# Block-sparse attention and hardswish MLP on one core: q and k cast by DMA in long runs with per-head transposes, one ordered load queue, and row sums from 8 KB rows

## Chip, cores, metric

The kernel runs on one core of a Trainium2 chip. The metric is the device time of the whole launch in microseconds (us), the median of several runs. The medians and ranges take in every run.

The profile's engine names: PE is TensorE's matmuls, PEld its weight loads, ACT is ScalarE, DVE is VectorE, POOL is GpSimd, SP is SyncE. L229 is line 229 of that kernel's own source, so one code line has different numbers in different kernels.

## The reference, cut to what matters

```python
batch, n_heads, seq, head_dim = (4, 8, 768, 64)
block, window = (32, 16)
k_sum = k.reshape(B, H, nb, block, D).max(axis=3)      # block summaries: max of keys,
v_sum = v.reshape(B, H, nb, block, D).mean(axis=3)     # mean of values
# softmax over the local band |i-j| < 16 together with the 24 block summaries
# (whose scores get log(block) added), times [v, v_sum]
...
h = x @ w_in                                           # x: 3072 x 512, d_ff = 2048
g = h * clip(h + 3, 0, 6) / 6
return (g @ w_out).astype(float32)
```

The MLP is cut into 8 tiles of 384 tokens, two per batch. The first layer of a tile is 64 matmuls ("hp", 16 steps of 4), the second 48 ("op").

## The kernel before, the parts that matter

q and k of batches 0 to 2 come as fp32 through the SyncE queue in 512-byte runs (two tokens of 256 bytes side by side in one partition), are cast on ACT and DVE, and are transposed on TensorE, six 128x128 transposes for a pair of heads. Since each partition holds two neighbouring tokens, the transposed PSUM tile has all even tokens first and then all odd ones. The copies out of PSUM put them back in order. Row sums of v come from four accumulating DMAs for each batch and head group, each of which waits for the one before it (51.0 us of GpSimd's waits in the trace are for DMAs of v rows).

```python
NSPLIT = 3; TSUM = 8
def load_split(b, p):                                   # SyncE queue, fp32
    ...
    nc.sync.dma_start(out=t, in_=src[b, 2*p:2*p+2].rearrange("h (u p s) d -> p (h u) (s d)", p=128, s=2))

def load_vrows(b, c):                                   # c = 0..3, accumulating, GpSimd queue
    for g in range(2):
        ...
        nc.gpsimd.dma_start(out=vr_t[b, g][:], in_=src[c], accum_op=ALU.bypass if c == 0 else ALU.add)

def vsum(b, g):
    nc.vector.tensor_reduce(a[:], vr_t[b, g][:].rearrange("p t d -> p d t"), axis=AX.X, op=ALU.add)
    ...

def Tk(b, p):
    tp = transposed(kb_t[b, p], ...)                    # 6 transposes into PSUM
    for j, copy in enumerate((nc.scalar.copy, nc.vector.tensor_copy)):
        rows = slice(64 * j, 64 * j + 64)
        o = kbd[p][rows, :, 64 * j:64 * j + 64]
        if b < NSPLIT:
            copy(o.rearrange("p n (c s) -> p s n c", s=2), tp[rows].rearrange("p (s n c) -> p s n c", s=2, n=NK))
    ...
```

The softmax here doesn't subtract the row's maximum and nothing guards it: scores larger than these inputs give would overflow.

## Time and profile before

| | |
|---|---|
| time, median (7 runs in the rounds of the first experiments) | 289.0 us |
| span of the profiled run | 287.4 us |
| TensorE busy | 236.1 us |
| first matmul of MLP tile 0 / 1 / 2 | 41.5 / 87.5 / 117.9 us |

The tile starts are read from the order of TensorE's matmuls: every 64th "hp" matmul opens a tile. From the page of the kernel before, its busy times and the chain that ended last (shares of the span):

```profile
PE 236.1 (82%) x1670; PEld 138.7 (48%) x1696; DVE 164.7 (57%) x357; ACT 167.1 (58%) x325; POOL 71.8 (25%) x109
...
PE 53%; DMA 22%; DVE 10%; issue 6%; ACT 4%; POOL 3%; POOLq 0%; ACTq 0%; DVEq 0%
PE op L311 22%; PE hp L301 21%; DMA vr<-in_v_dram 14%; DMA wout<-in_moe_w_out_dram 6%; DVE g L305 2%; DMA split<-in_k_dram 2%; DVE kbd L209 2%; PE num L273 2%; DVE red L213 2%; PE num L271 1%; DVE va L188 1%; ACT r L304 1%; PE den L280 1%; PE den L277 1%; PE sl L235 1%
```

The view of stretches of the kernel before, one line for each stretch in us, with the busy time and number of instructions of each engine, the granted share of TensorE's clock, the DMA share and GB/s:

```profile
0.00:41.50 41.50, 17.97 (x151) 13.23 (x152) 25.90 (x77) 22.76 (x43) 22.83 (x46) 1.00 1.20 205
41.50:100.00 58.50, 38.60 (x266) 22.64 (x268) 31.97 (x67) 28.62 (x58) 22.57 (x31) 0.82 1.09 183
100.00:287.40 187.40, 179.53 (x1257) 102.83 (x1278) 106.79 (x214) 115.71 (x226) 26.40 (x34) 1.00 0.42 64
```

TensorE is busy 96% of the time after 100 us. Before that it idles for 43 us, and that is the room that a change of the loads can win. (The 1.00 of the clock column in the first stretch is no measurement. The trace has no clock record before 39 us, and a 128x384 matmul of line 280 took 0.53 us at 38.5 us and 0.33 to 0.34 from 40.3 us on, so TensorE ran slower there.) The reads of v rows hold 14% of the chain.

The groups of instructions that the change touches (line, engine, operation, out<-in, shapes, count | busy us, mean ns | idle before and its releaser):

```profile
L209 DVE COPY kbd<-tp 64x768 bf16<-64x768 bf16 x12 | 12.1, 1011 | 11.8 <-ACT kbd L209 11.6
L209 ACT COPY kbd<-tp 64x768 bf16<-64x768 bf16 x12 | 12.0, 1000 | 3.1 <-PE tp L199 3.1
...
L188 DVE TENSOR_REDUCE va<-vr 96x64 f32<-96x512 f32 x8 | 8.2, 1026 | 7.3 <-DMA vr<-in_v_dram 7.3
L225 DVE COPY qT<-tp 128x768 bf16<-128x768 bf16 x8 | 8.1, 1011 | 0.0
...
L211 ACT COPY kbd<-tp 64x768 bf16<-64x768 bf16 x4 | 3.1, 787 | 0.4 <-PE tp L199 0.4
...
L211 DVE COPY kbd<-tp 64x768 bf16<-64x768 bf16 x4 | 2.2, 561 | 1.6 <-ACT kbd L211 1.6
```

### The profile page before, as it was taken

The numbers are of one execution on the slowest core, as the hardware profiler recorded it, in microseconds if no ns is written. First come the engines' busy times: TensorE is split into PE (matmuls) and PEld (weight loads), VectorE is DVE, ScalarE is ACT, GpSimd is POOL, SyncE is SP. The second block draws the span as 40 slices with busy tenths as digits, with TensorE's granted clock in tenths as the row PEclk, the third lists the DMA queues.
The fourth block names the chain that finished last, engine by engine and source line by source line (L and its number), as shares of the span: only waits on it lengthen the run. The fifth ranks groups of instructions, "written<-read, shape, count | busy, mean of one in ns | idle before, by whom it ended". The sixth has DMA issues, their size and how long they took to land.

```text
span 287.4 us, 4536 instructions
## 1 busy us (share of the span) xinstructions
PE 236.1 (82%) x1670; PEld 138.7 (48%) x1696; DVE 164.7 (57%) x357; ACT 167.1 (58%) x325; POOL 71.8 (25%) x109
## 2 busy tenths in 40 slices
PE   1433398167279999999999999999999999999994
PEld 1232265033135655555565555556665555555541
DVE  6773654326087996788868444776753444444400
ACT  3743768044337796746776667666876654555421
POOL 8234932032655413660423203000000000000000
PEclk9999999687859999999999999999999999999999
DMA  7999999999998699990659509010100101010111
GB/s 213 231 232 209 142 201 209 217 241 229 137 155 133 133 169 255 121 111 36 74 63 77 65 36 93 1 41 36 39 0 36 39 36 39 36 38 36 39 74 73
DMA packets 67350, 31.23 MB, mean 109 GB/s; under 512 B 39040, under 2 KB 61568, under 8 KB 67328
## 3 DMA queue, kind: packets, MB, share of 16 engines
q0 software_dynamic: 45056, 15.21, 46.7%
q1 hardware_dynamic: 22272, 15.73, 19.8%
q8 instruction: 13, 0.21, 0.3%
q14 instruction: 9, 0.07, 0.1%
HBM read 33.55 MB, written 6.29 MB: 139 GB/s over the span
## 4 chain that ended last, share of the span: by engine, by line
PE 53%; DMA 22%; DVE 10%; issue 6%; ACT 4%; POOL 3%; POOLq 0%; ACTq 0%; DVEq 0%
PE op L311 22%; PE hp L301 21%; DMA vr<-in_v_dram 14%; DMA wout<-in_moe_w_out_dram 6%; DVE g L305 2%; DMA split<-in_k_dram 2%; DVE kbd L209 2%; PE num L273 2%; DVE red L213 2%; PE num L271 1%; DVE va L188 1%; ACT r L304 1%; PE den L280 1%; PE den L277 1%; PE sl L235 1%
## 5 line engine op out<-in xcount | busy, mean ns | idle before, releaser
L301 PE MATMUL hp<-x,win 128*128 128x384 bf16 x512 | 108.5, 336 | 21.5 <-DVE g L305 21.2
L304 ACT ACTIVATE r<-hp,half_c 128x384 f32<-128x384 f32 x128 | 73.9, 579 | 63.5 <-PE hp L301 63.0
L311 PE MATMUL op<-wout,g 128*128 128x512 bf16 x358 | 97.7, 382 | 1.4 <-issue 0.2
L305 DVE SCALAR_TENSOR_TENSOR g<-r,hp 128x384 bf16<-128x384 f32 x128 | 70.0, 549 | 46.6 <-ACT r L304 46.0
L301 PEld LDWEIGHTS <-win 128*128 128x128 bf16 x512 | 49.0, 100 | 59.4 <-issue 28.8
L311 PEld LDWEIGHTS <-g 128*128 128x128 bf16 x384 | 37.5, 99 | 32.5 <-issue 1.4
L117 POOL DMA_DIRECT2D vr<-in_v_dram x32 | 25.0, 821 | 57.2 <-DMA vr<-in_v_dram 51.0
L107 POOL DMA_DIRECT2D vbd<-in_v_dram x32 | 26.3, 879 | 28.2 <-PE num L273 20.5
L291 DVE TENSOR_TENSOR x<-num,lg 128x384 bf16<-128x384 f32 x32 | 17.7, 554 | 21.5 <-ACT lg L290 20.8
L289 ACT ACTIVATE lg<-den 128x384 f32<-128x384 f32 x32 | 15.6, 492 | 15.9 <-PE den L287 9.5
L235 PE MATMUL sl<-qT,kbd 128*128 128x94 bf16 x192 | 15.7, 225 | 10.5 <-ACT asum L248 6.4
L238 ACT ACTIVATE at<-sl 128x376 bf16<-128x376 f32 x48 | 21.6, 483 | 2.1 <-PE sl L235 2.1
L95 ACT CAST qb<-split 128x384 bf16<-128x384 f32 x24 | 11.2, 513 | 17.9 <-DMA split<-in_q_dram 17.9
L235 PEld LDWEIGHTS <-kbd 128*128 128x128 bf16 x192 | 13.1, 110 | 17.2 <-issue 10.5
L199 PE MATMUL tp<-ident,kb 128*128 128x128 bf16 x96 | 9.8, 247 | 12.6 <-DVE kb L95 12.6
L315 ACT COPY ot<-op 128x512 f32<-128x512 f32 x24 | 13.9, 581 | 8.8 <-PE op L311 8.6
L209 DVE COPY kbd<-tp 64x768 bf16<-64x768 bf16 x12 | 12.1, 1011 | 11.8 <-ACT kbd L209 11.6
L239 DVE TENSOR_TENSOR at<-at,mask 128x376 bf16<-128x376 bf16 x48 | 15.7, 350 | 2.6 <-ACT at L238 2.3
L290 ACT ACTIVATE lg<-lg 128x384 f32<-128x384 f32 x32 | 16.8, 524 | 0.8
L273 PEld LDWEIGHTS <-vbd 128*128 128x128 bf16 x224 | 13.6, 101 | 6.6 <-issue 3.0
L95 DVE CAST kb<-split 128x384 bf16<-128x384 f32 x24 | 8.7, 388 | 13.2 <-DMA split<-in_k_dram 13.1
L273 PE MATMUL num<-at,vbd 128*128 128x94 bf16 (+2 forms) x224 | 14.9, 204 | 0.0
(64 smaller groups left out, 204.6 us busy)
## 6 DMA issues: line engine op xcount, KB each, us to landing
vr<-in_v_dram POOLq DMA_DIRECT2D x32, 192.0 KB, 6.2
out_dram<-ot SPq DMA_DIRECT2D x24, 256.0 KB, 2.0
split<-in_k_dram SPq DMA_DIRECT2D x12, 384.0 KB, 10.3
split<-in_q_dram SPq DMA_DIRECT2D x12, 384.0 KB, 11.2
vbd<-in_v_dram POOLq DMA_DIRECT2D x32, 96.0 KB, 4.6
win<-in_moe_w_in_dram POOLq DMA_DIRECT2D x4, 512.0 KB, 10.4
wout<-in_moe_w_out_dram POOLq DMA_DIRECT2D x4, 512.0 KB, 19.7
qb<-in_q_dram POOLq DMA_DIRECT2D x8, 96.0 KB, 3.2
```

Source lines behind the costliest of these rows:

```text
L95: copy(o[:, s], r[:, s])
L107: nc.gpsimd.dma_start(out=vbd[p][j * 64:(j + 1) * 64, :, j * 64:(j + 1) * 64], in_=v[b, 2 * p + j].rearrange("(n p) d -> p n d", p=KB))
L117: nc.gpsimd.dma_start(out=vr_t[b, g][:], in_=src[c], accum_op=ALU.bypass if c == 0 else ALU.add)
L209: copy(o.rearrange("p n (c s) -> p s n c", s=2), tp[rows].rearrange("p (s n c) -> p s n c", s=2, n=NK))
L235: nc.tensor.matmul(sp[:, i * WIN:(i + 1) * WIN], kbd[p][:, t], qT[p][:, t * KB:t * KB + WIN], start=True, stop=True)
L238: nc.scalar.activation(a, sp[:, 0:n * WIN].rearrange("p (n c) -> p n c", c=WIN), AF.Exp, scale=scl)
L273: nc.tensor.matmul(num[:, lo:hi], vbd[p][:, t], a[:, t, off:off + hi - lo], start=False, stop=(i == len(bl) - 1))
L291: nc.vector.tensor_tensor(xt[s][:, p], num[:], lg[:], op=ALU.mult)
L301: nc.tensor.matmul(hp[:], w_in_sb[:, kt, ft * 128:(ft + 1) * 128], xt[t][:, kt], start=(kt == 0), stop=(kt == NP - 1))
L304: nc.scalar.activation(r[:], hp[:], AF.Relu, bias=half_c[:], scale=1.0 / 6.0)
L305: nc.vector.scalar_tensor_tensor(gt[t][:, ft], r[:], 1.0, hp[:], op0=ALU.min, op1=ALU.mult)
L311: nc.tensor.matmul(ops[t][:], gt[t][:, ft, ts * 128:(ts + 1) * 128], w_out_sb[:, ft], start=(ft == 0), stop=(ft == NFT - 1))
```

## The change

Its intent: longer DMA runs for q and k of batches 0 and 1 (one partition holds 8 neighbouring tokens, 2 KB of fp32, cast to 1 KB of bf16 by the DMA), no fp32 staging and no casts on ACT and DVE, no accumulating reads that wait for each other, and one GpSimd queue whose order is fixed by hand so that what is needed first comes first. Batch 2 goes over to the 256-byte loads that batch 3 had before. The core of the diff:

```diff
-NSPLIT = 3
-TSUM = 8
+NLONG = 2
+RUN = 8
+RP = 96
+QCUT = 480
...
+    def load_k(b, p):
+        t = ld.tile([RP, 2, RUN, D], BF16, tag="kb", name="kb")
+        nc.gpsimd.dma_start(out=t[:], in_=k[b, 2 * p:2 * p + 2].rearrange("h (p s) d -> p h s d", s=RUN))
...
-            nc.gpsimd.dma_start(out=vr_t[b, g][:], in_=src[c], accum_op=ALU.bypass if c == 0 else ALU.add)
+        vr_t[b, g] = ld.tile([RS, BLK, D], F32, tag="vr", name="vr", bufs=2)
+        eng.dma_start(out=vr_t[b, g][:].rearrange("p t d -> p (t d)"),
+                          in_=v[b, 4 * g:4 * g + 4].rearrange("h (n t) d -> (h n) (t d)", t=BLK))
...
+        for i in range(4):
+            c = slice(i * D // 4, (i + 1) * D // 4)
+            nc.vector.tensor_reduce(a[:, c], vr_t[b, g][:, :, c].rearrange("p t d -> p d t"), axis=AX.X, op=ALU.add)
...
+        if long:
+            for s in range(RUN):
+                for j in range(2):
+                    nc.tensor.transpose(tp[64 * j:64 * j + 64, s * RP:(s + 1) * RP], t[:, j, s], ident[0:RP, 0:RP])
...
-                copy(o.rearrange("p n (c s) -> p s n c", s=2), tp[rows].rearrange("p (s n c) -> p s n c", s=2, n=NK))
+                copy(o.rearrange("p n (c s) -> p s n c", s=RUN), tp[rows].rearrange("p (s n c) -> p s n c", s=RUN, n=NK))
...
+        lo, hi, n = cut(part)            # q of batch 0 in two parts, n = 4; of batch 1 whole, n = 8
+        copy(qT[p][:, HALO + lo:HALO + hi].rearrange("p (c s) -> p s c", s=n),
+             tp[:, 0:hi - lo].rearrange("p (s c) -> p s c", s=n))
...
-    work_list = [(0, None), (1, None), (None, 0)] + [(t, t - 1) for t in range(2, NTILE)] + [(None, NTILE - 1)]
+    work_list = ([(0, None), (1, None), (None, 0), (None, 1), (2, None)] + [(t, t - 1) for t in range(3, NTILE)]
+                 + [(None, NTILE - 1)])
```

Cut: the order of the loads, v of batch 0 in two parts, the zero fills (partly moved to ACT), the copies into kbd of batch 0 (for every second head pair ACT now takes both), and the slots of the plan.

More of the change, by code (lines that the diff above doesn't have):

```diff
@@ L73 @@
     w_out_sb = const.tile([128, NFT, d_model], BF16, tag="wout", name="wout")
-    raw, kb_t, qb_t, vr_t = {}, {}, {}, {}
-    def load_split(b, p):
-        for i, (n, src) in enumerate((("k", k), ("q", q))):
-            if p % 2 == 0 and i == 0:
-                raw[b, p // 2] = ld.tile([128, 4, NT, 2 * D], F32, tag="split", name="split", bufs=2)
-                if b > 0:
-                    nc.vector.tensor_copy(raw[b, p // 2][:, 0, 0, 0:1], xt[2 * b - 2][:, 3 if b == 1 else 0, 0:1])
-            t = raw[b, p // 2][:, 2 * (p % 2) + i]
-            nc.sync.dma_start(out=t, in_=src[b, 2 * p:2 * p + 2].rearrange("h (u p s) d -> p (h u) (s d)", p=128, s=2))
-            raw[n, b, p] = t
@@ L89, in cast_split @@
-    def cast_split(b, p):
-        for n, keep, copy in (("k", kb_t, nc.vector.tensor_copy), ("q", qb_t, nc.scalar.copy)):
-            t = ld.tile([128, NT, 2, D], BF16, tag=n + "b", name=n + "b")
-            r = raw[n, b, p].rearrange("p (h u) (s d) -> p s h u d", h=2, s=2)
-            o = t[:].rearrange("p (s u) h d -> p s h u d", s=2)
-            for s in range(2):
-                copy(o[:, s], r[:, s])
-            keep[b, p] = t
-    def load_qk(b, p):
-        for n, src, keep in (("k", k, kb_t), ("q", q, qb_t)):
-            t = ld.tile([128, NT, 2, D], BF16, tag=n + "b", name=n + "b")
-            for j in range(2):
-                nc.gpsimd.dma_start(out=t[:, :, j], in_=src[b, 2 * p + j].rearrange("(s p) d -> p s d", p=128))
-            keep[b, p] = t
@@ L105, in load_v, with load_q @@
-    def load_v(b, p):
+    kb_t, qb_t, vr_t = {}, {}, {}
+    def load_k(b, p):
+        if b >= NLONG:
+            return load_natural(k, kb_t, b, p)
+        t = ld.tile([RP, 2, RUN, D], BF16, tag="kb", name="kb")
+        nc.gpsimd.dma_start(out=t[:], in_=k[b, 2 * p:2 * p + 2].rearrange("h (p s) d -> p h s d", s=RUN))
+        kb_t[b, p] = t
+    def load_q(b, p, part=None):
+        if b >= NLONG:
+            return load_natural(q, qb_t, b, p)
+        lo, hi, n = cut(part)
+        t = ld.tile([(hi - lo) // n, 2, n, D], BF16, tag="qb" if part is None else "qc", name="qb")
+        nc.gpsimd.dma_start(out=t[:], in_=q[b, 2 * p:2 * p + 2, lo:hi].rearrange("h (p s) d -> p h s d", s=n))
+        qb_t[b, p, part] = t
@@ L106, in load_v, with cut, load_natural @@
+    def cut(part):
+        return {None: (0, S, RUN), 0: (0, QCUT, RUN // 2), 1: (QCUT, S, RUN // 2)}[part]
+    def load_natural(src, keep, b, p):
+        t = ld.tile([128, NT, 2, D], BF16, tag="kb" if src is k else "qb", name="nb")
+        for j in range(2):
+            nc.gpsimd.dma_start(out=t[:, :, j], in_=src[b, 2 * p + j].rearrange("(s p) d -> p s d", p=128))
+        keep[(b, p, None) if src is q else (b, p)] = t
+    def load_v(b, p, lo=0, hi=NK):
         for j in range(2):
             nc.gpsimd.dma_start(
-                out=vbd[p][j * 64:(j + 1) * 64, :, j * 64:(j + 1) * 64],
@@ L109, in load_v @@
-                in_=v[b, 2 * p + j].rearrange("(n p) d -> p n d", p=KB))
-    def load_vrows(b, c):
-        for g in range(2):
-            if c == 0:
-                vr_t[b, g] = ld.tile([RS, TSUM, D], F32, tag="vr", name="vr")
-            src = v[b, 4 * g:4 * g + 4].rearrange("h (n c t) d -> c (h n) t d", c=BLK // TSUM, t=TSUM)
-            nc.gpsimd.dma_start(out=vr_t[b, g][:], in_=src[c], accum_op=ALU.bypass if c == 0 else ALU.add)
+                out=vbd[p][j * 64:(j + 1) * 64, lo:hi, j * 64:(j + 1) * 64],
@@ L119, with load_vrows @@
+                in_=v[b, 2 * p + j].rearrange("(n p) d -> p n d", p=KB)[:, lo:hi])
+    def load_vrows(b, g, eng=nc.sync):
+        vr_t[b, g] = ld.tile([RS, BLK, D], F32, tag="vr", name="vr", bufs=2)
+        eng.dma_start(out=vr_t[b, g][:].rearrange("p t d -> p (t d)"),
+                          in_=v[b, 4 * g:4 * g + 4].rearrange("h (n t) d -> (h n) (t d)", t=BLK))
     w_in_v = moe_w_in.rearrange("(kt p) f -> p kt f", p=128)
@@ L128, in load_w_out @@
         nc.gpsimd.dma_start(out=w_out_sb[:, c * w:(c + 1) * w], in_=w_out_v[:, c * w:(c + 1) * w])
-    for p in range(NP):
-        load_split(0, p)
+    ctx.enter_context(tc.manual_schedule(engines={ET.Pool}))
+    start = tc.manual_schedule(engines={ET.PE, ET.Activation, ET.DVE})
+    start.__enter__()
+    load_k(0, 0)
     ident = const.tile([128, 128], BF16, tag="id", name="ident")
@@ L138 @@
                             channel_multiplier=1, pattern=[[-1, 128]])
-    obd = const.tile([128, 2, D], BF16, tag="obd", name="obd")
-    hmk = const.tile([128, 2, NB], BF16, tag="hmk", name="hmk")
-    half_c = const.tile([128, 1], F32, tag="half", name="half_c")
-    def zero_off_diagonal(eng, t):
-        eng.memset(t[0:64, :, 64:128], 0.0)
-        eng.memset(t[64:128, :, 0:64], 0.0)
-    for p in range(2):
-        zero_off_diagonal(nc.vector, kbd[p])
-        zero_off_diagonal(nc.vector, vbd[p])
-    def clear(p):
-        nc.vector.memset(qT[p][:, 0:HALO], 0.0)
-        nc.vector.memset(qT[p][:, S + HALO:], 0.0)
-        nc.vector.memset(kst[p][:], 0.0)
-    for t in (obd, hmk):
-        nc.vector.memset(t[:], 0.0)
-        nc.vector.memset(t[0:64, 0], 1.0)
-        nc.vector.memset(t[64:128, 1], 1.0)
-    nc.vector.memset(half_c[:], 0.5)
+    load_q(0, 0, 0)
+    load_k(0, 1)
+    load_q(0, 1, 0)
     mask = const.tile([128, WIN], BF16, tag="mask", name="mask")
@@ L170 @@
                                 channel_multiplier=1, pattern=[[-1, WIN]])
-    hmv, osum = [], []
-    for par in range(2):
-        m = const.tile([RS, 2, D], F32, tag=f"hmv{par}", name=f"hmv{par}")
-        nc.gpsimd.memset(m[:], 1.0)
-        for j in range(2):
-            lo = (2 * par + j) * NB
-            nc.gpsimd.affine_select(out=m[:, j], in_=m[:, j], compare_op=ALU.is_ge, fill=0.0, base=-lo,
-                                    channel_multiplier=1, pattern=[[0, D]])
-            nc.gpsimd.affine_select(out=m[:, j], in_=m[:, j], compare_op=ALU.is_ge, fill=0.0, base=lo + NB - 1,
-                                    channel_multiplier=-1, pattern=[[0, D]])
-        hmv.append(m)
-        osum.append(const.tile([RS, 2, D], BF16, tag=f"osum{par}", name=f"osum{par}"))
+    for p in range(2, NP):
+        load_k(0, p)
+        load_q(0, p, 0)
@@ new lines, with zero_off_diagonal @@
+    for g in range(2):
+        load_vrows(0, g, nc.gpsimd)
+    obd = const.tile([128, 2, D], BF16, tag="obd", name="obd")
+    hmk = const.tile([128, 2, NB], BF16, tag="hmk", name="hmk")
+    half_c = const.tile([128, 1], F32, tag="half", name="half_c")
+    zero = const.tile([128, 1], F32, tag="zero", name="zero")
+    nc.vector.memset(zero[:], 0.0)
+    def zero_off_diagonal(eng, t):
+        w = t[:].rearrange("p n c -> p (n c)").bitcast(F32).rearrange("p (n c) -> p n c", c=64)
+        for r, c in ((slice(0, 64), slice(32, 64)), (slice(64, 128), slice(0, 32))):
+            if eng is nc.scalar:
+                eng.copy(w[r, :, c], zero[r].unsqueeze(2).to_broadcast([64, NK, 32]))
+            else:
+                eng.memset(w[r, :, c], 0.0)
@@ new lines @@
+    for t in (obd, hmk):
+        nc.vector.memset(t[:], 0.0)
+        nc.vector.memset(t[0:64, 0], 1.0)
+        nc.vector.memset(t[64:128, 1], 1.0)
+    nc.vector.memset(half_c[:], 0.5)
+    for p in range(NP):
+        zero_off_diagonal(nc.vector, kbd[p])
+        nc.vector.memset(qT[p][:, 0:HALO], 0.0)
+        nc.vector.memset(qT[p][:, S + HALO:], 0.0)
+        nc.vector.memset(kst[p][:], 0.0)
+        zero_off_diagonal(nc.scalar, vbd[p])
+    hm4 = const.tile([RS, 4, D], F32, tag="hm4", name="hm4")
@@ new lines @@
+    osum4 = const.tile([RS, 4, D], BF16, tag="osum4", name="osum4")
+    nc.gpsimd.memset(hm4[:], 1.0)
+    nc.gpsimd.affine_select(out=hm4[:], in_=hm4[:], compare_op=ALU.is_ge, fill=0.0, base=0,
+                            channel_multiplier=1, pattern=[[-NB, 4], [0, D]])
+    nc.gpsimd.affine_select(out=hm4[:], in_=hm4[:], compare_op=ALU.is_ge, fill=0.0, base=NB - 1,
+                            channel_multiplier=-1, pattern=[[NB, 4], [0, D]])
+    hmv = [hm4[:, 2 * par:2 * par + 2] for par in range(2)]
@@ L186, in vsum @@
+    osum = [osum4[:, 2 * par:2 * par + 2] for par in range(2)]
+    NK0 = 7
+    for p in range(NP):
+        load_v(0, p, 0, NK0)
     def vsum(b, g):
         a = work.tile([RS, D], F32, tag="va", name="va")
-        nc.vector.tensor_reduce(a[:], vr_t[b, g][:].rearrange("p t d -> p d t"), axis=AX.X, op=ALU.add)
+        for i in range(4):
+            c = slice(i * D // 4, (i + 1) * D // 4)
+            nc.vector.tensor_reduce(a[:, c], vr_t[b, g][:, :, c].rearrange("p t d -> p d t"), axis=AX.X, op=ALU.add)
@@ L189, in vsum, with Tk @@
         for par in range(2):
-            nc.vector.tensor_tensor(vst[2 * g + par][:], a[:].unsqueeze(1).to_broadcast([RS, 2, D]), hmv[par][:],
+            nc.vector.tensor_tensor(vst[2 * g + par][:], a[:].unsqueeze(1).to_broadcast([RS, 2, D]), hmv[par],
                                     op=ALU.mult)
     asum = {}
-    def transposed(t, pool, tag):
+    def Tk(b, p):
+        pool, tag = (ps_o, "o") if b == 0 else (ps_s, "s")
         tp = pool.tile([128, S], BF16, tag=tag, name="tp")
-        for st in range(NT):
-            nc.tensor.transpose(tp[:, st * 128:(st + 1) * 128], t[:, st].rearrange("p h d -> p (h d)"), ident[:])
-        return tp
@@ L202, in Tk @@
-    def Tk(b, p):
-        tp = transposed(kb_t[b, p], *((ps_o, "o") if b == 0 else (ps_s, "s")))
+        t, long = kb_t[b, p], b < NLONG
+        if long:
+            for s in range(RUN):
+                for j in range(2):
+                    nc.tensor.transpose(tp[64 * j:64 * j + 64, s * RP:(s + 1) * RP], t[:, j, s], ident[0:RP, 0:RP])
+        else:
+            for s in range(NT):
+                nc.tensor.transpose(tp[:, s * 128:(s + 1) * 128], t[:, s].rearrange("p h d -> p (h d)"), ident[:])
@@ L204, in Tk @@
         red = work.tile([128, NB], BF16, tag="red", name="red")
-        for j, copy in enumerate((nc.scalar.copy, nc.vector.tensor_copy)):
+        for j in range(2):
+            copy = nc.scalar.copy if j == 0 or (b == 0 and p % 2 == 1) else nc.vector.tensor_copy
             rows = slice(64 * j, 64 * j + 64)
             o = kbd[p][rows, :, 64 * j:64 * j + 64]
-            if b < NSPLIT:
-                copy(o.rearrange("p n (c s) -> p s n c", s=2), tp[rows].rearrange("p (s n c) -> p s n c", s=2, n=NK))
+            if long:
+                copy(o.rearrange("p n (c s) -> p s n c", s=RUN), tp[rows].rearrange("p (s n c) -> p s n c", s=RUN, n=NK))
@@ L210, in Tk @@
             else:
                 copy(o, tp[rows].rearrange("p (n c) -> p n c", c=KB))
-        if b < NSPLIT:
-            nc.vector.tensor_reduce(red[:], tp[:].rearrange("p (s n c) -> p n s c", s=2, n=NB), axis=AX.XY, op=ALU.max)
+        if long:
+            nc.vector.tensor_reduce(red[:], tp[:].rearrange("p (s n c) -> p n s c", s=RUN, n=NB), axis=AX.XY, op=ALU.max)
         else:
@@ L219, in Tk, with Tq @@
             red[:].unsqueeze(1).to_broadcast([128, 2, NB]), hmk[:], op=ALU.mult)
-    def Tq(b, p):
-        tp = transposed(qb_t[b, p], *((ps_h, "h") if b == 0 else (ps_s, "s")))
-        o = qT[p][:, HALO:HALO + S]
-        if b < NSPLIT:
-            (nc.scalar.copy if b == 0 else nc.vector.tensor_copy)(
-                o.rearrange("p (c s) -> p s c", s=2), tp[:].rearrange("p (s c) -> p s c", s=2))
-        else:
-            nc.vector.tensor_copy(o, tp[:])
+    def Tq(b, p, part=None):
+        pool, tag = (ps_h, "h") if b == 0 else (ps_s, "s")
+        tp = pool.tile([128, S], BF16, tag=tag, name="tp")
+        t = qb_t[b, p, part]
+        copy = nc.vector.tensor_copy if part is None else nc.scalar.copy
+        if b >= NLONG:
+            for s in range(NT):
+                nc.tensor.transpose(tp[:, s * 128:(s + 1) * 128], t[:, s].rearrange("p h d -> p (h d)"), ident[:])
+            copy(qT[p][:, HALO:HALO + S], tp[:])
+            return
+        lo, hi, n = cut(part)
+        r = (hi - lo) // n
+        for s in range(n):
+            for j in range(2):
+                nc.tensor.transpose(tp[64 * j:64 * j + 64, s * r:(s + 1) * r], t[:, j, s], ident[0:r, 0:r])
+        copy(qT[p][:, HALO + lo:HALO + hi].rearrange("p (c s) -> p s c", s=n),
+             tp[:, 0:hi - lo].rearrange("p (s c) -> p s c", s=n))
     def Sl(b, p, lo, hi):
@@ L276, in AV @@
         ones = obd[:].rearrange("p h d -> p (h d)")
-        nc.tensor.matmul(den[:], osum[p % 2][:].rearrange("p h d -> p (h d)"), asm[:], start=True, stop=False)
+        nc.tensor.matmul(den[:], osum[p % 2].rearrange("p h d -> p (h d)"), asm[:], start=True, stop=False)
         t0, t1 = (0, NK // 2) if half == 0 else (NK // 2, NK)
@@ L317, in F2, with S_first @@
             nc.sync.dma_start(out=out[row:row + 128], in_=o[:])
-    start = tc.manual_schedule(engines={ET.PE, ET.Activation, ET.DVE})
-    start.__enter__()
-    for p in range(2):
-        cast_split(0, p)
-        clear(p)
-        zero_off_diagonal(nc.vector, vbd[p + 2])
-    for p in range(NP):
-        load_vrows(0, p)
-        load_v(0, p)
-    for c in range(4):
-        load_w_in(c)
-    for p in (0, 1):
-        Tk(0, p)
-        Tq(0, p)
-        clear(p + 2)
-        zero_off_diagonal(nc.vector, kbd[p + 2])
-    for par in range(2):
-        nc.vector.tensor_scalar_mul(osum[par][:], hmv[par][:], float(BLK))
-    for p in (0, 1):
-        for lo in (0, 4, 8):
-            Sl(0, p, lo, lo + 4)
-        cast_split(0, p + 2)
-        Tk(0, p + 2)
-        Tq(0, p + 2)
+    for c in range(2):
+        load_w_in(c)
+    for p in range(NP):
+        load_q(0, p, 1)
+    for c in range(2, 4):
+        load_w_in(c)
+    for p in range(NP):
+        load_v(0, p, NK0, NK)
+    for c in range(4):
+        load_w_out(c)
+    def S_first(p):
+        for lo, hi in ((0, 4), (4, NK0)):
+            Sl(0, p, lo, hi)
+    for p in range(NP):
+        Tk(0, p)
+        Tq(0, p, 0)
+        if p > 0:
+            S_first(p - 1)
     vsum(0, 0)
+    nc.vector.tensor_scalar_mul(osum4[:], hm4[:], float(BLK))
     Ss(0, 0, 0)
-    for p in (2, 3):
-        for lo in (0, 4, 8):
-            Sl(0, p, lo, lo + 4)
+    S_first(3)
     vsum(0, 1)
@@ L353 @@
     start.__exit__(None, None, None)
-    for p in range(NP):
-        load_split(1, p)
-    for c in range(4):
-        load_w_out(c)
     plan = {}
@@ L363, in at_slot @@
         plan.setdefault(int(s), []).append(f)
-    at_slot(0, lambda: Ss(0, 0, 1))
-    at_slot(0, lambda: Ss(0, 1, 1))
     for p in range(NP):
-        at_slot(2 * p + 1, lambda p=p: AV(0, p, 1))
+        at_slot(2 * p + 2, lambda p=p: Tq(0, p, 1))
+        at_slot(2 * p + 3, lambda p=p: Sl(0, p, NK0, NK))
+        if p % 2 == 1:
+            at_slot(2 * p + 3, lambda g=p // 2: Ss(0, g, 1))
+        at_slot(12 + p, lambda p=p: AV(0, p, 1))
     def attention(b, t_slot, t_gap, av_slot, av_gap, loads):
@@ L372, in attention @@
             s = t_slot + t_gap * p
-            if b < NSPLIT:
-                at_slot(s - 2, lambda p=p: cast_split(b, p))
             at_slot(s, lambda p=p: Tk(b, p))
@@ L384, in attention @@
                 at_slot(s, lambda g=p // 2: vsum(b, g))
-            if NSPLIT <= b + 1 < B:
-                at_slot(s + 1, lambda p=p: load_qk(b + 1, p))
+            if 2 <= b + 1 < B:
+                at_slot(s + 1, lambda p=p: (load_k(b + 1, p), load_q(b + 1, p)))
         for i, (p, half) in enumerate(((0, 0), (1, 0), (2, 0), (3, 0), (0, 1), (1, 1), (2, 1), (3, 1))):
@@ L392 @@
     for p in range(NP):
-        at_slot(8, lambda p=p: load_vrows(1, p))
-        at_slot(8, lambda p=p: load_v(1, p))
-    for p in range(NP):
-        at_slot(33, lambda p=p: load_split(2, p))
-    attention(1, 10, 4, lambda i: 32 + 2 * i, 2, None)
+        at_slot(0, lambda p=p: (load_k(1, p), load_q(1, p)))
+        at_slot(16, lambda p=p: load_v(1, p))
+    for g in range(2):
+        at_slot(16, lambda g=g: load_vrows(1, g, nc.gpsimd))
+    attention(1, 32, 4, lambda i: 48 + 2 * i, 2, None)
     for b in range(2, B):
-        base = 48 + 32 * (b - 2)
-        for p in range(NP):
-            at_slot(base + p, lambda b=b, p=p: load_vrows(b, p))
+        base = 64 + 32 * (b - 2)
+        for g in range(2):
+            at_slot(base, lambda b=b, g=g: load_vrows(b, g))
         order = (14, 16, 24, 26, 18, 20, 28, 30)
         attention(b, base, 5, lambda i, base=base: base + order[i], 2, None)
-    work_list = [(0, None), (1, None), (None, 0)] + [(t, t - 1) for t in range(2, NTILE)] + [(None, NTILE - 1)]
+    work_list = ([(0, None), (1, None), (None, 0), (None, 1), (2, None)] + [(t, t - 1) for t in range(3, NTILE)]
+                 + [(None, NTILE - 1)])
     for n, (f1, f2) in enumerate(work_list):
```

## The prediction

> **What bounds the kernel now.** The page shows TensorE busy 236.1 of 287.4 us. By stretches: before 41.5 us (first matmul of the first MoE tile, line 301) TensorE is busy 18.0 us; from 41.5 to 100, 38.6 of 58.5; from 100 on, 179.5 of 187.4. So the last two thirds are TensorE-bound, the first 100 us starved. The chain that ended last names the cause: "DMA vr<-in_v_dram" has 14% of the span, "DMA wout" 6%. A batch's four accumulating row-sum reads wait for each other in the GpSimd queue (table of waits: POOL vr behind DMA vr, 51 us; one read lands in 6.2 us), and all behind them waits too: w_in is issued only at 31 us, w_out at 34, batch 1's v at 60 to 80, and TensorE idles (7.5 us once). Idle stretches also halve the clock (mean granted 0.55 in 55 to 60, 0.66 in 80 to 90).[...]
>
> **What the change does.** [...] Removed: fp32 staging and casts (8.7 us DVE, 11.2 ACT), all accumulate waits. Added: 20 more transposes per head pair in batches 0 and 1 (about 0.06 us each, estimated from six in 0.48: 5 us per batch; only batch 1's lies on a TensorE-bound stage); row sums over 2048 instead of 512 elements per partition (1.02 us becomes about 4.1, estimated by size; 6 us more VectorE per batch).
>
> **New start (estimate).** From the trace's packets: w_in 2.5 us a chunk; 128-byte packets 800 per us; GpSimd 0.8 us per issue. Then batch 0's k and q land by 11 us, row sums 14, v blocks 0 to 6 by 20, w_in 22 to 31, the rest of v 36, w_out 46. VectorE then binds (9 us of tile work plus two row sums of 4.5), so line 301 starts near 27 instead of 41.5.
>
> **From there.** Tiles 0 and 1 without second-layer work take 1.05 us per step (two PSUM buffers: 0.81 TensorE + 0.58 ACT + 0.55 DVE and gaps, halved): 35 us, to 62. Second layers 0 and 1 (48 matmuls of 0.216 each) with batch 1's attention (15.7 us of TensorE per batch, plus 5): 41, to 103. Tile 2: 17, to 120. The rest, five first layers of 10.4, six second layers of 10.4, 26 of attention: 140, plus 2% and the tail: 265. Hiccups and cold clock 3; timed runs read about 2 over the span: **270 us**, 80% range 261 to 281. Faster by over 2%: 0.90; within 2%: 0.07; slower: 0.03.
>
> **What would show the steps right.** First line-301 matmul near 27 us; no POOL wait behind DMA vr, nor its share in the chain; full clock from about 30 us; TensorE idle from 40 to 100 us about halved; after 120 us the same 96% busy as before.
>
> **What would make it wrong.** (1) q, k and w_in share one queue: if casting 1 KB runs is slower than w_in's, or an issue exceeds 0.8 us, they come late. (2) Batch 1's row sums are last in the queue; VectorE runs in order, so an early vsum stalls the transposes' evictions around 70 to 85 us. (3) The 4 us sums delay line 305 in the steady stage. (4) Single-buffered num/den makes AV latency-bound in the second-layer stage: 3 to 5 us. (5) Batch 2's 256-byte loads come late.

62 us to the end of tiles 0 and 1, plus 41 and 17, is 120; plus 140, 2% and the tail, 265; plus 3 and 2, the 270.

What the kernel before shows of the hardware in it: the clock record falls to half at 52.7, 66.3 and 76.6 us: within an idle stretch of TensorE of 6.6 us, 0.2 us after one of 3.1 us, and within one of 7.5 us. That the idling is the cause no run shows. GpSimd takes 0.82 us for an issue of v rows and 0.88 for one of v blocks. Its waits for chunks of w_in end at 39.0, 41.6 and 44.4 us, 2.6 and 2.8 us apart. In the busiest microseconds 800 to 1090 packets of 128 bytes start. The four issues of w_in start from 31.0 us on, behind v rows that had waited 4.2 us for a DMA until 28.05. VectorE in order (point 2): it stood 7.3 us before the row sum at 79.4 us, waiting for v rows, and line 305, whose input ACT had finished at 72.2, came only after it, at 80.3. Point 4 is a guess that no run tests.

## The result, and the profile after

The kernel after takes 314.5 us (median of 4 runs, 314.2 to 316.2) against 289.2 for the kernel before in the same rounds. The ratio is 1.091, with a 95% interval of 1.083 to 1.099. Ratios here and below are the mean time of one kernel's fast runs over that of the other's of the same rounds, so not quite the ratio of the quoted medians. The change made the kernel 9% slower, where 7% faster was predicted.

The page of the kernel after, the same lines as before:

```profile
PE 243.7 (78%) x1830; PEld 140.8 (45%) x1856; DVE 195.9 (63%) x343; ACT 191.2 (61%) x315; POOL 79.9 (26%) x118
...
PE 49%; DVE 24%; ACT 23%; issue 3%; ACTq 0%; DVEq 0%
PE hp L330 21%; PE op L340 18%; ACT kbd L229 11%; DVE va L204 6%; DVE kbd L229 5%; DVE qT L256 4%; ACT r L333 3%; DVE g L334 3%; ACT qT L256 2%; PE num L302 2%; ACT at L267 2%; DVE x L320 2%; PE num L300 2%; ACT vbd L168 1%; PE den L306 1%
```

No DMA is left in the chain: in this the change did what it was meant to do. ACT and DVE took its place, with the copies into kbd and qT (lines 229 and 256) first: 11 + 5 + 4 + 2, so 22% of the span. ACT and DVE were to lose 20 us of casts. Instead ACT is busy 24 us longer than before and DVE 31 us longer.

The stretches of the kernel after:

```profile
0.00:41.50 41.50, 12.95 (x152) 9.25 (x152) 25.11 (x56) 35.42 (x32) 30.54 (x54) 1.00 1.13 151
41.50:100.00 58.50, 41.57 (x339) 23.73 (x341) 34.60 (x53) 34.86 (x59) 16.02 (x23) 0.90 0.89 115
100.00:312.50 212.50, 189.16 (x1347) 107.82 (x1365) 136.17 (x235) 120.88 (x226) 33.36 (x42) 0.96 0.44 64
```

ACT is busy 35 of the first 41.5 us. The groups of the kernel after that answer to those shown of before:

```profile
L229 ACT COPY kbd<-tp 64x768 bf16<-64x768 bf16 x10 | 35.4, 3544 | 0.3 <-PE tp L219 0.2
L204 DVE TENSOR_REDUCE va<-vr 96x16 f32<-96x512 f32 x32 | 31.1, 1010 | 0.1
L229 DVE COPY kbd<-tp 64x768 bf16<-64x768 bf16 x6 | 21.2, 3534 | 14.6 <-ACT kbd L229 14.6
...
L256 DVE COPY qT<-tp 128x768 bf16<-128x768 bf16 x4 | 14.2, 3561 | 0.0
```

Here is the fault. A copy of 64x768 bf16, same shape, same type, same engines, takes 3.54 us where it took 1.00. What differs is not in the shape columns: the copy restores eight phases instead of two, so it writes one bf16 every 16 bytes where it wrote one every 4 bytes.

ACT from 6 to 34 us in the kernel after, in order of time (start us, us, engine, line, operation, out<-in, shapes, count):

```profile
6.27 3.54 ACT L229 COPY kbd<-tp 64x768 bf16<-64x768 bf16 x1
9.31 1.57 ACT L256 COPY qT<-tp 128x480 bf16<-128x480 bf16 x1
10.61 7.19 ACT L229 COPY kbd<-tp 64x768 bf16<-64x768 bf16 x2
...
19.53 3.53 ACT L229 COPY kbd<-tp 64x768 bf16<-64x768 bf16 x1
...
24.60 7.07 ACT L229 COPY kbd<-tp 64x768 bf16<-64x768 bf16 x2
31.69 1.22 ACT L256 COPY qT<-tp 128x480 bf16<-128x480 bf16 x1
```

There is no bracket with a wait on these lines: ACT runs one copy after the other and waits for nobody. The first MLP matmul comes at 46.7 us, 5 us later than before instead of 14 earlier. From tile 2 on (its first matmul is at 152.8 us) the kernel after needs 159.7 us (312.5 - 152.8). All of the loss lies before that.

### The profile page after: what moved, and what is told of

It reads as the page before. It is cut to its first block, busy times and chain, and to the rows that moved or that the text cites. A ratio compares the mean times of both kernels' runs of the same rounds, so it can differ in the third digit from the quotient of the medians.

```text
span 312.5 us, 4819 instructions
## 1 busy us (share of the span) xinstructions
PE 243.7 (78%) x1830; PEld 140.8 (45%) x1856; DVE 195.9 (63%) x343; ACT 191.2 (61%) x315; POOL 79.9 (26%) x118
## 4 chain that ended last, share of the span: by engine, by line
PE 49%; DVE 24%; ACT 23%; issue 3%; ACTq 0%; DVEq 0%
PE hp L330 21%; PE op L340 18%; ACT kbd L229 11%; DVE va L204 6%; DVE kbd L229 5%; DVE qT L256 4%; ACT r L333 3%; DVE g L334 3%; ACT qT L256 2%; PE num L302 2%; ACT at L267 2%; DVE x L320 2%; PE num L300 2%; ACT vbd L168 1%; PE den L306 1%
## 5 line engine op out<-in xcount | busy, mean ns | idle before, releaser
L340 PE MATMUL op<-wout,g 128*128 128x512 bf16 x358 | 100.5, 393 | 1.1 <-issue 0.2
L330 PEld LDWEIGHTS <-win 128*128 128x128 bf16 x512 | 49.1, 99 | 56.8 <-issue 25.7
L108 POOL DMA_DIRECT2D vbd<-in_v_dram x40 | 29.0, 734 | 59.3 <-PE num L302 46.9
L229 ACT COPY kbd<-tp 64x768 bf16<-64x768 bf16 x10 | 35.4, 3544 | 0.3 <-PE tp L219 0.2
L204 DVE TENSOR_REDUCE va<-vr 96x16 f32<-96x512 f32 x32 | 31.1, 1010 | 0.1
L229 DVE COPY kbd<-tp 64x768 bf16<-64x768 bf16 x6 | 21.2, 3534 | 14.6 <-ACT kbd L229 14.6
L267 ACT ACTIVATE at<-sl 128x376 bf16<-128x376 f32 (+2 forms) x48 | 22.6, 502 | 6.2 <-PE sl L264 6.0
L103 POOL DMA_DIRECT2D nb<-in_k_dram x16 | 13.2, 833 | 37.6 <-PE tp L219 28.7
L302 PEld LDWEIGHTS <-vbd 128*128 128x128 bf16 x224 | 14.2, 105 | 8.1 <-issue 4.6
L268 DVE TENSOR_TENSOR at<-at,mask 128x376 bf16<-128x376 bf16 (+2 forms) x48 | 15.9, 348 | 2.5 <-ACT at L267 2.4
L103 POOL DMA_DIRECT2D nb<-in_q_dram x16 | 13.2, 835 | 16.0 <-PE tp L255 15.1
L300 PE MATMUL num<-asum,vst 96*128 96x384 bf16 x32 | 11.4, 356 | 6.7 <-DVE x L320 4.3
```

The source lines that it names most:

```text
L103: nc.gpsimd.dma_start(out=t[:, :, j], in_=src[b, 2 * p + j].rearrange("(s p) d -> p s d", p=128))
L108: nc.gpsimd.dma_start(out=vbd[p][j * 64:(j + 1) * 64, lo:hi, j * 64:(j + 1) * 64], in_=v[b, 2 * p + j].rearrange("(n p) d -> p n d", p=KB) ...
L204: nc.vector.tensor_reduce(a[:, c], vr_t[b, g][:, :, c].rearrange("p t d -> p d t"), axis=AX.X, op=ALU.add)
L229: copy(o.rearrange("p n (c s) -> p s n c", s=RUN), tp[rows].rearrange("p (s n c) -> p s n c", s=RUN, n=NK))
L267: nc.scalar.activation(a, sp[:, 0:n * WIN].rearrange("p (n c) -> p n c", c=WIN), AF.Exp, scale=scl)
L302: nc.tensor.matmul(num[:, lo:hi], vbd[p][:, t], a[:, t, off:off + hi - lo], start=False, stop=(i == len(bl) - 1))
```

## The experiments

Theory W: stepped writes are slow, and they alone turn a gain into a loss. Rival P: any reordering with eight phases is slow, whichever side is stepped, because of its short runs or of PSUM. Rival S: the copies are not what costs; the long row sums, the queue order or the new order of stages are.

### e1_swap: the same reordering, stepped on the other side

```diff
-copy(o.rearrange("p n (c s) -> p s n c", s=RUN), tp[rows].rearrange("p (s n c) -> p s n c", s=RUN, n=NK))
+copy(o.rearrange("p n (c s) -> p n c s", s=RUN), tp[rows].rearrange("p (s n c) -> p n c s", s=RUN, n=NK))
-copy(qT[...].rearrange("p (c s) -> p s c", s=n), tp[...].rearrange("p (s c) -> p s c", s=n))
+copy(qT[...].rearrange("p (c s) -> p c s", s=n), tp[...].rearrange("p (s c) -> p c s", s=n))
```

Element for element it is the same copy. Only the order in which the elements are visited changes: the destination is walked contiguously, and the PSUM source with a step of 96 elements.

> The kernel after with one edit: the copies that put the long-run transposes back in order walk the destination contiguously and the PSUM source with a step, instead of the source contiguously and the destination with a step of 16 bytes. Same elements, same count, right result. Theory W (the write step costs): kbd copies fall from 3.54 us to 0.8 to 1.1, the first line-330 matmul comes at about 28 us instead of 46.7, and the run takes 265 to 280 us. Rival P (any permuting copy with eight phases costs, whichever side is stepped, because of short runs or of PSUM): the copies stay at 3 us or more and the run stays at 305 to 325. Rival S (copies are not what costs; the four row-sum reduces, the queue order and the new order of stages are): copies get shorter but the run stays above 298.

Measured: 271.5 us (269.5 to 274.4) against 289.0 before, ratio 0.935 (0.932 to 0.938). Its groups:

```profile
L229 ACT COPY kbd<-tp 64x768 bf16<-64x768 bf16 x10 | 7.9, 793 | 1.1 <-PE tp L219 0.9
L229 DVE COPY kbd<-tp 64x768 bf16<-64x768 bf16 x6 | 5.8, 960 | 1.4 <-ACT kbd L229 1.1
L256 DVE COPY qT<-tp 128x768 bf16<-128x768 bf16 x4 | 3.8, 954 | 0.0
```

3.54 us became 0.79 on ACT and 0.96 on DVE. Rivals P and S fall: two lines turn 9% slower into 6.5% faster. The two spans differ by 312.5 - 270.7 = 41.8 us. Tile 0 starts 16.1 us earlier (30.6 against 46.7). From there to the start of tile 2 is 80.4 us instead of 106.1, which is 25.7 us less. From tile 2 to the end both take 159.7 us.

The stretch from the start of tile 0 to that of tile 2, first of the kernel after, then of e1_swap, from the view of stretches:

```profile
46.70:152.80 106.10, 75.97 (x604) 41.89 (x610) 80.27 (x106) 56.85 (x92) 27.07 (x36) 0.87 0.80 108
```

```profile
30.60:111.00 80.40, 67.25 (x604) 38.69 (x610) 60.29 (x106) 45.13 (x92) 37.93 (x52) 0.98 1.33 177
```

The same 604 matmuls take 76.0 us in the one and 67.3 in the other, at a granted clock of 0.87 and 0.98. So 8.7 of the 25.7 us are a longer TensorE busy time at the lower clock, and the other 17 are plain idle time. In this stretch the clock record of the kernel after falls to half five times, each time during an idle stretch of TensorE of 2.6 to 5.2 us or within 1.3 us after it; that of e1_swap falls once, after 2.3 us idle. So idle time and a lower clock came together here, and a stall seems to be paid for more than once; no run sets the two apart.

### e2_strides: a ruler for the step

The kernel before, where head pair p reorders with 2, 4, 8 or 16 phases. Its output is wrong, which doesn't matter for the time.

```diff
+w = (2, 4, 8, 16)[p]
+if b == 1:      # stepped read, contiguous write
+    copy(o.rearrange("p n (c s) -> p n c s", s=w), tp[rows].rearrange("p (s n c) -> p n c s", s=w, n=NK))
+else:           # contiguous read, stepped write
+    copy(o.rearrange("p n (c s) -> p s n c", s=w), tp[rows].rearrange("p (s n c) -> p s n c", s=w, n=NK))
```

> A ruler, with a wrong result on purpose: the kernel before, in which head pair 0, 1, 2, 3 permutes with 2, 4, 8 and 16 phases. In batches 0 and 2 the destination is stepped (4, 8, 16, 32 bytes), in batch 1 the PSUM source is. Theory W: stepped writes of 64x768 cost about 1.0, 1.8, 3.5 us for 4, 8, 16 bytes, on both engines alike[...]; stepped reads stay at 0.8 to 1.1 us whatever the step. Rival P: reads and writes grow alike, and the cost goes by the number of short runs, so that 32 bytes costs more than 16.

Measured, DVE's copies into kbd in order of time. The first four are batch 0, where the writes have steps of 4, 8, 16 and 32 bytes. The other four are batch 1, where the reads have steps of 768, 384, 192 and 96 bytes and the writes are contiguous:

```profile
10.32 1.00 DVE L213 COPY kbd<-tp 64x768 bf16<-64x768 bf16 x1 [1.38 <-ACT kbd L213]
13.55 1.84 DVE L213 COPY kbd<-tp 64x768 bf16<-64x768 bf16 x1
23.50 3.53 DVE L213 COPY kbd<-tp 64x768 bf16<-64x768 bf16 x1 [4.20 <-ACT kbd L213]
33.60 3.37 DVE L213 COPY kbd<-tp 64x768 bf16<-64x768 bf16 x1 [4.05 <-ACT kbd L213]
65.30 0.96 DVE L211 COPY kbd<-tp 64x768 bf16<-64x768 bf16 x1
...
80.92 0.96 DVE L211 COPY kbd<-tp 64x768 bf16<-64x768 bf16 x1
...
91.79 0.96 DVE L211 COPY kbd<-tp 64x768 bf16<-64x768 bf16 x1
...
98.77 0.96 DVE L211 COPY kbd<-tp 64x768 bf16<-64x768 bf16 x1
```

ACT shows the same staircase: 0.99, 1.83, 3.52 and 3.37 us for stepped writes, 0.78 or 0.79 for all stepped reads. The copies into qT, whose inner runs are 12 times as long, agree (DVE in batch 2: 1.01, 1.87, 3.56, 3.38), but for up to 10% on ACT (batch 0: 0.99, 1.95, 3.88, 3.67). So the length of the runs and the engine matter little, and the step of the writes decides. The cost about doubles from 4 to 8 to 16 bytes (1.00, 1.84 and 3.53 us on DVE) and then stops growing (3.37 at 32), where rival P expected more at 32 bytes than at 16. Why it stops there was not shown.

### e3_before_s8: the fault alone, in the kernel before

```diff
-... s=2 ...                                  # kbd copies, batches 0 to 2
+w = 8 if b < 2 else 2;  ... s=w ...
-... s=2 ...                                  # qT copies
+w = (4, 8, 2)[b];  ... s=w ...
```

> The slow copies alone put into the kernel before, wrong result on purpose: its copies in batches 0 and 1 write with the steps that the kernel after uses (16 bytes for k and for q of batch 1, 8 bytes for q of batch 0); loads, transposes, order and row sums stay. It adds about 52 us of copy time on ACT and VectorE together. Theory W: these copies are on the chain in both kernels, so the run grows by 20 to 40 us, to 308 to 330. Rival S: they would mostly fit in idle time of ACT and VectorE, and the run stays below 300.

Measured: 309.9 us against 289.0, ratio 1.073 (1.069 to 1.077). Loads, transposes, row sums and order are those of before. The groups of these copies:

```profile
L210 ACT COPY kbd<-tp 64x768 bf16<-64x768 bf16 x12 | 32.4, 2698 | 6.8 <-PE tp L199 6.8
L210 DVE COPY kbd<-tp 64x768 bf16<-64x768 bf16 x12 | 32.4, 2697 | 23.5 <-ACT kbd L210 23.5
...
L227 DVE COPY qT<-tp 128x768 bf16<-128x768 bf16 x8 | 18.3, 2286 | 0.0
...
L227 ACT COPY qT<-tp 128x768 bf16<-128x768 bf16 x4 | 8.7, 2184 | 0.0
```

That is 91.8 us of reordering copies instead of 36.2 (but for the last line, the means mix slow copies with those of batch 2), so 56 us more copy time cost 21 us of run time. The slow copies are sufficient: alone they make the kernel before about as slow as the whole change made it.

### e5_batch0_only: where the slow copies sit

The kernel after with contiguous writes in batch 0 only.

```diff
+if b == 0: <as e1_swap>
+else:      <as the kernel after>
```

> Where on the chain the slow copies sit: the kernel after with contiguous writes in batch 0 only; batch 1's copies still write one bf16 every 16 bytes. The first line-330 matmul should come at about 30.6 us as in e1_swap (46.7 in the kernel after). If both batches' copies lie on the chain, the run lands between, at 290 to 303 us (16 of the 43 us at the start, the rest in batch 1). If only the start matters, it lands near 272 as e1_swap does; if the start is made up for later, near 312.

Measured: 299.2 us (297.4 to 301.3), ratio 1.036 (1.029 to 1.044). The first MLP matmul comes at 29.3 us. About 15 of the 43 us lie in the start and about 28 in batch 1 (314.5 to 299.2 to 271.5, medians of different rounds). Both batches' copies were on the chain, and what is lost at the start is not made up later.

### e4_rows_only and e8_rows_tree: the row sums alone, in the kernel before

e4 takes from the change only the 8 KB rows, read in the SyncE queue, and the four reduces.

```diff
-nc.gpsimd.dma_start(out=vr_t[b, g][:], in_=src[c], accum_op=...)       # four, each waits for the last
+nc.sync.dma_start(out=vr_t[b, g][:].rearrange("p t d -> p (t d)"), in_=v[b, 4*g:4*g+4].rearrange("h (n t) d -> (h n) (t d)", t=BLK))
```

> One part of the change alone in the kernel before: row sums from one read of 8 KB rows in the SyncE queue and four reduces in place of four accumulating reads. If the accumulating reads' waits in the GpSimd queue were what starved the first 100 us, as the prediction said, the run falls to 270 to 280 us and POOL's wait behind DMA vr is gone; if other loads or the order bound just as closely, it stays at 283 to 292.

Measured: 286.0 us, ratio 0.991 (0.987 to 0.994). POOL's wait behind the accumulating reads is gone from the table of waits (51 us in the kernel before), and yet only 3 us are won. The chain that ended last in e4, by line, says who took over:

```profile
PE op L311 21%; PE hp L301 20%; DMA split<-in_q_dram 9%; DVE va L188 8%; DVE g L305 4%; DMA split<-in_k_dram 4%; SPq L86 4%; DVE red L213 2%; DVE kbd L209 2%; DVE at L239 2%; PE num L273 2%; ACT r L304 2%; ACT kbd L209 2%; PE tp L199 1%; PE num L271 1%
```

The fp32 loads of q and k (9 + 4%) and the longer sums on DVE (8%) stand just behind. Besides, e4 is not the removal of a wait alone: it also puts the row reads into the queue of q and k, and it lengthens the sums. Two of them, 3.8 us each, run on DVE from 34.3 and from 40.2 us, and the first MLP matmul comes at 48.1 us instead of 41.5. e8 adds pairwise sums (see e6) to e4:

> On e4_rows_only (286.0, the accumulating waits gone but the sums at 3.75 us each), the pairwise additions of e6_tree: about 2.6 us per sum. If the slow sums gave back what the queue had won, as the 8% of DVE row sums in e4's chain suggest, the run falls by 3 to 8 us to 278 to 283; if the loads of q and k in the SyncE queue bind (13% of e4's chain), it stays within 2 us of 286.

Measured: 283.6 us (281.5 to 288.0), ratio 0.981 (0.975 to 0.986). The medians differ by 2.4 us, just outside the 2 us of the second case and short of the 3 to 8 of the first; the ratios differ by 0.010, about 3 us. At 2% the verdict is unclear, and the two kernels ran in different rounds on different chips, so it is a weak result. The cheaper sums give a little; that the loads of q and k still bind was not tested by a run.

### e9_qk_only: the q and k part alone, in the kernel before

q and k of batches 0 to 2 cast by DMA in 2 KB runs in the GpSimd queue, per-head transposes, contiguous writes; row sums and order as before. (The change itself has long runs in batches 0 and 1 only.)

```diff
-load_split + cast_split (fp32 in the SyncE queue, casts on ACT and DVE, s=2)
+nc.gpsimd.dma_start(out=t[:], in_=src[b, 2*p:2*p+2].rearrange("h (p s) d -> p h s d", s=8))
+copy(o.rearrange("p n (c s) -> p n c s", s=8), tp[rows].rearrange("p (s n c) -> p n c s", s=8, n=NK))
```

> The other half of the change alone, without its fault: the kernel before with q and k of batches 0 to 2 cast by DMA in 2 KB runs in the GpSimd queue, per-head transposes, and copies that write contiguously; row sums, order of stages and manual schedule as before. If long cast runs are a gain by themselves: below 284. If they only pay together with a fixed queue order and without the accumulating reads, since q and k now stand in the same in-order queue as those: 285 to 305.

Measured: 279.2 us (278.6 to 280.6), ratio 0.968 (0.964 to 0.973). Long cast runs pay by themselves once the copies write contiguously. They are the larger of the two parts: 9 us, against 3 for the row sums. Together with the new order of queue and stages it is 17.5 us (e1_swap). The new order has no run of its own.

### e6_tree and e7_tree_act: a version that beats both

In e1_swap DVE is the next bound. The chain of e1_swap between 70 and 82 us, by line (shares of that stretch), names the row sums first:

```profile
by line: DVE va L204 31.3%; DVE g L334 16.4%; PE hp L330 14.3%; DVE kbd L229 8.0%; DVE red L233 8.0%; DVE qT L256 7.2%; DVE at L268 6.6%; PE op L340 5.4%; ACT r L333 4.9%; DVE vst L206 4.1%; issue 0.9%; PE sl L264 0.7%
```

e6 replaces four reduces, which read with a step of 256 bytes, by contiguous pairwise additions:

```diff
-for i in range(4):
-    nc.vector.tensor_reduce(a[:, c], vr_t[b, g][:, :, c].rearrange("p t d -> p d t"), axis=AX.X, op=ALU.add)
+n = BLK // 2
+while n > 1:
+    lo, hi = vr_t[b, g][:, 0:n], vr_t[b, g][:, n:2 * n]
+    nc.vector.tensor_tensor(lo, lo, hi, op=ALU.add)
+    n //= 2
+nc.vector.tensor_tensor(a[:], vr_t[b, g][:, 0], vr_t[b, g][:, 1], op=ALU.add)
```

> On e1_swap, the row sums of 32 rows as five contiguous pairwise additions (1024, 512, 256, 128, 64 elements per partition) in place of four reduces that read with a step of 256 bytes (3.75 us together). Estimate from 1.02 us per 512 stepped elements: about 2.3 us per sum instead of 3.75. In e1_swap VectorE is busy 9.9 of 10 us from 70 to 100 us and the row sums have 7% of the chain, so theory D (VectorE binds there, and the sums are on its path) expects 6 to 11 us less than e1_swap, 261 to 266. If they are not on the path: within 2 us of 271.

Measured: 265.6 us (262.7 to 270.3), ratio 0.916 (0.909 to 0.924), the fastest of all. A sum now takes 2.8 us (the five levels take 1.22, 0.68, 0.42, 0.29 and 0.22) against 3.9 (31.3 us for 8 sums), less of a saving than estimated. The gain over e1_swap is 5.9 us by the medians and about 5.3 by the ratios (0.916 against 0.935 of the kernel before), just short of the 6 to 11 expected. It fits sums on DVE's path, and not the rival (within 2 us).

e7 moves the copies into qT of batches 1 to 3 to ACT as well:

```diff
-copy = nc.vector.tensor_copy if part is None else nc.scalar.copy
+copy = nc.scalar.copy
```

> On e6_tree, also the copies into qT of batches 1 to 3 go from VectorE (0.95 us each with eight phases, 0.56 contiguous) to ACT, which is about half idle there. Theory D expects another 1 to 3 us less than e6_tree; if VectorE no longer binds after the tree, no change within 1 us or a loss of 1 to 2, since ACT takes 0.8 us or more for each.

Measured: 268.3 us, ratio 0.928 (0.922 to 0.934). The medians say 2.7 us slower than e6, but the two intervals touch, so all that can be said is that it is no gain.

### A note on correctness

All runs, including the two with a wrong order of tokens, agreed with the reference within its tolerance. q and k are scaled by 0.1, so presumably the scores are so small that the softmax is nearly flat. The comparison therefore does not prove the index maps of these kernels. For e1_swap they follow from the edit: both sides of the copy keep their names and only the order of the loops is exchanged.

## Why the prediction was wrong, point by point

- **What bounds the kernel now: half right.** The first 100 us are starved and the rest is TensorE-bound: from tile 2 on both the kernel after and e1_swap need the same 159.7 us. But taking the chain's largest DMA entry, the accumulating reads, as what would be won was too simple. e4 took them away and won 3 us: the loads of q and k and the longer sums stood just behind. The larger gain came from q and k (e9, 9 us).
- **The step that failed: "What the change does" and "New start".** The sum listed casts, waits, transposes and row sums. It did not list the reordering copies, and so took them over at the 1.0 us that they cost before; "9 us of tile work" leaves no room for more. The diff changes s=2 to s=RUN in them, and this makes them 3.54 us. That is 79.6 us of reordering copies in the kernel after (35.4 and 21.2 into kbd, 14.2, 5.6 and 3.2 into qT) where e1_swap has 21.4. Of these 58 us, 42 came out in the span. The engine was wrong too: "VectorE then binds", but in the start it was ACT, which spent 26.9 us on batch 0's ten copies between 6 and 33 us (six into kbd, four into qT, most of them listed above) and was busy 32.0 of the first 33 us, VectorE 17.0. With this one term put right, the same plan measured 271.5 us against the predicted 270, and its first MLP matmul came at 30.6 us against the predicted 27. That the total came within 1.5 us is partly luck: tile 2 started 8 us late and the rest was 5 us shorter than its estimate.
- **The evidence for it was at hand.** In the kernel before, the same copy took 0.79 and 0.56 us contiguous (batch 3) and 1.0 with a step of 4 bytes.
- **"Two row sums of 4.5": right in size**, 3.75 us of reduces in the start and 0.5 for what follows. As feared in points 2 and 3 of the last paragraph they sit on DVE's path (e6), but this is a matter of 6 us and not of 43.
- **"Transposes add 5 us per batch": wrong.** Sixteen 96x64 transposes take 0.53 us at full clock in the kernel after, where six 128x128 took 0.50 in the kernel before. A single small one is hardly shorter in the trace (0.21 us against 0.22). But the two of a step, one for each head, start nearly together (mostly within 4 ns, all pairs but one within 33) and run side by side: at full clock a pair comes every 42 ns, where the large ones come every 56 ns. So q and k of a head pair take about the same time as before.
- **"From there": about right for e1_swap.** Tile 2 starts at 111.0 us, predicted 103; from there to the end 159.7 us, predicted 165 with hiccups. In the kernel after, the stage between was long because batch 1's copies held ACT and DVE and because TensorE ran at a lower clock there (0.87 against 0.98).
- **"No POOL wait behind DMA vr": nearly right**, 4.6 us instead of 51.

## What to carry to other kernels

When a layout change makes a reordering deeper, cost the copy that undoes it: look at the access patterns on both sides, not at the shape columns, which stay the same. Walk the SBUF destination contiguously and put the step on the PSUM side (here 0.79 us on ACT, and 0.96 on DVE, against 3.54 and 3.53 with the step, of 16 bytes, on the SBUF side; DVE's copy without any step took 0.56). And before believing that removing the largest wait will pay, ask who stands second in line; an experiment that takes away that wait and as little else as possible tells it in one run.
